# Attention scores of batches 2 to 7 as per-head float32 products on 32x32 array tiles

## The chip, the cores and the metric

The kernel runs on one core of a Trainium2 chip. The metric is device time in microseconds (us) of one execution; lower is better. A core has five engines that work side by side, each on its own in-order list of instructions: PE (TensorE, the matrix engine; PEld is its weight loads), DVE (VectorE), ACT (ScalarE), POOL (GpSimd) and SP (SyncE, which here issues the DMAs). PE multiplies a stationary operand, loaded into a 128x128 array, with a moving operand that streams past it, and writes its sums to PSUM, which has eight banks of 512 float32 words per partition. A smaller product can be placed on part of the array: on a group of rows (the partitions that it reads) and a group of columns (the partitions that it writes).

## The reference

```python
def sm_attn(qq, kk, vv):
    s = scale * np.matmul(qq, kk.transpose(0, 1, 3, 2))
    s = s - np.max(s, axis=-1, keepdims=True)
    a = np.exp(s)
    a = a / (np.sum(a, axis=-1, keepdims=True) + 1e-09)
    return np.matmul(a, vv)
p_packed = sm_attn(p, k, v)              # p: 32 rows per head; q, k, v: 576 rows per head
out = sm_attn(q, p_packed, p_packed)
...
xn = x / rms * rms_g                     # x: 4608 tokens x 512 (8 heads x 64)
y = (silu(xn @ w_gate) * (xn @ w_val)) @ w_out       # 512 -> 1536 -> 512
h = y @ w_in                                         # 512 -> 2048
out = np.maximum(0.01 * h, h) @ w_out2               # 2048 -> 512
```

There are 8 batches and 8 heads of dimension 64. Two products of each head are called scores here: p with k (32 x 576, "s1") and q with the packed result P (576 x 32, "s2").

## The kernel before

Attention is done in 16 units of one batch b and one half u of the heads (four heads). A unit has two parts. `soft1` (s1) loads k and p, turns them on DVE (`keys`, `packs`), makes the scores with PE, then exponents on ACT, and the packed result on PE (`packed`); `packed_turn` turns that for the second part. `soft2` (s2) loads and turns q (`queries`), makes the scores against P and goes on to the attention weights, the squares for the norm and the factors of the first MLP.

The 576 tokens stand as 32 partitions per head and 18 blocks: partition 32h+t holds 18 consecutive tokens of head h. DVE's transpose works on 32x32 blocks in place, so after it partition 32h+d holds dimension d of head h, in two halves j of 32 dimensions. A score contracts over these partitions. Four heads at once on the full array need a block-diagonal stationary operand: `packs` multiplies p by a 0/1 mask on POOL (`pm`) and transposes 128x256; `packed` writes P through a mask to `Pm` and `packed_turn` transposes that to `PT`. The tokens are taken in two chunks c of nine blocks (288 columns), one PSUM bank each, so a score is four float32 matmuls (two chunks by two halves j) of 128x128 by 288 columns (L312 for s1, L470 for s2). A float32 matmul shows in the trace as two records, each with a weight load.

In odd batches the heads of a pair stand swapped: `load_rows` loads them in four DMAs of 32 partitions instead of one. Later steps rely on that order of the output rows.

The first MLP follows in 96 steps of (hidden block, batch of a pair, chunk): g and v (L143, up to six matmuls each per half), then y. These are float32r products in three terms (high and low halves). The attention of later batches is hung into these steps by tables of slot numbers (`ONE`, `TWO`), four slots to a step. Batches 0 and 1 are done ahead of the first step (slots below 0), batches 2 to 7 within the steps. A scheduler then orders each engine's instructions by program order and by its own estimate of when each can start; PSUM tiles of tag "y" (four banks) serve y, the scores, `ta`, `pp` (the packed result) and the `fold` products alike.

`fold` (L888) folds the norm's gain and P into the MLP weights. It already works on small tiles: 64x32, eight at once (four column groups by two row groups), 512 columns, into two banks; `claim` ahead of it writes 16 columns into the first of the two banks (L867), so that the eight start together. `packed` (L367) works on four tiles of 96x32, 64 columns, six products summed on each tile.

The branches for `i >= FAST` and `i >= FASTQ` never run: both are 16 and i ends at 15.

Of the kernel before, what the change touches and what calls it, by code (L numbers as in the profile page):

```python
# [8 lines left out]
F32 = mybir.dt.float32  # L9
# [40 lines left out]
WBUFS = 8  # L50
FAST = 16
FASTQ = 16
OWN = 1
# [15 lines left out]
def pack_attention_moe_kernel(  # L69
# [125 lines left out]
    def load_rows(dst, src, b, u):  # L195
# [5 lines left out]
        return ins  # L201

    raw = {}

    def load_k(b, u):
        t = att.tile([P, NS, 2, T], F32, tag="raw", bufs=raws, name=f"k{b}{u}")
        last = load_rows(t.rearrange("p s j t -> p (s j t)"), kf, b, u)
        tp = att.tile([P, D], F32, tag="praw", bufs=2, name=f"p{b}{u}")
        load_rows(tp, pf, b, u)
        raw["k", b, u] = t  # L210
        raw["p", b, u] = tp
        return last
# [7 lines left out]
    def load_q(b, u):  # L220
        t = att.tile([P, NS, 2, T], F32, tag="raw", bufs=raws, name=f"q{b}{u}")
        load_rows(t.rearrange("p s j t -> p (s j t)"), qf, b, u)
        raw["q", b, u] = t
# [31 lines left out]
    def soft1(i):  # L255
# [4 lines left out]
        def keys():  # L260
            kr = raw.pop(("k", b, u))
            st["kT"] = att.tile([P, NS, 2, T], F32, tag="tr", bufs=2, name="kT" + nm)
            nc.vector.transpose(
                out=st["kT"].rearrange("p s j t -> p (s j t)"),
                in_=kr.rearrange("p s j t -> p (s j t)"),
            )
            if i >= FAST:
                st["kh"] = att.tile([P, NS, 2, T], F32R, tag="raw", bufs=raws, name="kh" + nm)
                st["kl"] = att.tile([P, NS, 2, T], F32R, tag="tr", bufs=2, name="kl" + nm)
                split(st["kT"], st["kh"], st["kl"])  # L270
            if i + 1 < NU:
                last = load_k(*divmod(i + 1, 2))
            if i == 0:
                with tc.issue_after(last.ins):
                    for f_ in weights[HOLD:]:
                        f_()

        def packs():
            pr_ = raw.pop(("p", b, u))
            pm = att.tile([P, 4, D], F32, tag="pm", bufs=1, name="pm" + nm)  # L280
            nc.gpsimd.tensor_tensor(
                out=pm, in0=pr_.unsqueeze(1).to_broadcast([P, 4, D]), in1=mask, op=ALU.mult
            )
            st["pT"] = att.tile([P, 2, 4, NPK], F32, tag="pT", bufs=2, name="pT" + nm)
            nc.vector.transpose(out=st["pT"], in_=pm.rearrange("p h (j d) -> p j h d", j=2))
            if i >= FAST:
                st["ph"] = att.tile([P, 2 * P], F32R, tag="pm", bufs=1, name="ph" + nm)
                st["pl"] = att.tile([P, 2 * P], F32R, tag="pT", bufs=2, name="pl" + nm)
                split(st["pT"].rearrange("p j h k -> p (j h k)"), st["ph"], st["pl"])

        def scores():
            e1 = st["e1"] = att.tile([P, T, NS], F32, tag="e1", bufs=1, name="e1" + nm)
            ev = e1.rearrange("p t (c s) -> p c s t", c=2)
            mx = att.tile([P, 2], F32, tag="mx", bufs=2, name="mx" + nm)
            parts = banks("s1" + nm, b)
            for n, (s1, cs) in enumerate(parts):
                for k_, c in enumerate(cs):
                    if i >= FAST:
                        ss = slice(c * CS, (c + 1) * CS)
                        mm3(  # L300
                            s1[:, k_, :CH],
                            [
                                (
                                    (st["ph"][:, j * P : j * P + P], st["pl"][:, j * P : j * P + P]),
                                    (st["kh"][:, ss, j, :], st["kl"][:, ss, j, :]),
                                )
                                for j in range(2)
                            ],
                        )
                        continue  # L310
                    for j in range(2):
                        nc.tensor.matmul(  # L312
                            s1[:, k_, :CH],
                            lhsT=st["pT"][:, j].rearrange("p h k -> p (h k)"),
                            rhs=st["kT"][:, c * CS : (c + 1) * CS, j, :],
                            start=j == 0,
                            stop=j == 1,
                        )
# [42 lines left out]
        def packed():  # L361
            vr = raw.pop(("v", b, u))
            pp = bank("pp" + nm)
            for j in range(NJ):
# [20 lines left out]

        def packed_turn():
            PT = att.tile([P, 2, 4, NPK], F32, tag="PT", bufs=2, name="PT" + nm)
            Pj = st["Pm"].rearrange("p h (j d) -> p j h d", j=2)
# [5 lines left out]
            raw["P", b, u] = (st["Pm"], PT)  # L394
            if i >= FAST:
                Ph = att.tile([P, 2 * P], F32R, tag="Ph", bufs=2, name="Ph" + nm)
                Pl = att.tile([P, 2 * P], F32R, tag="PT", bufs=2, name="Pl" + nm)
                split(PT.rearrange("p j h k -> p (j h k)"), Ph, Pl)
                raw["P", b, u] = (st["Pm"], (Ph, Pl))

# [19 lines left out]
    def soft2(i):  # L420
# [14 lines left out]
        def queries(cs):  # L435
# [6 lines left out]
            if cs[-1] == 1:  # L442
                raw.pop(("q", b, u))
                if i >= FAST:
                    st["qh"] = att.tile([P, NS, 2, T], F32R, tag="raw", bufs=raws, name="qh" + nm)
                    st["ql"] = att.tile([P, NS, 2, T], F32R, tag="tr", bufs=2, name="ql" + nm)
                    split(qT, st["qh"], st["ql"])
                if i + 1 < NU:
                    load_q(*divmod(i + 1, 2))

        def scores(cs):
            Pm, PT = raw["P", b, u]
            sn = tile_of("sn", "sn", [P, NS, NPK])
            for s2, cs in banks("s2" + nm, b):
                for k_, c in enumerate(cs):
                    if i >= FAST:
                        ss = slice(c * CS, (c + 1) * CS)
                        mm3(
                            s2[:, k_, :CH],
                            [  # L460
                                (
                                    (PT[0][:, j * P : j * P + P], PT[1][:, j * P : j * P + P]),
                                    (st["qh"][:, ss, j, :], st["ql"][:, ss, j, :]),
                                )
                                for j in range(2)
                            ],
                        )
                        continue
                    for j in range(2):
                        nc.tensor.matmul(  # L470
                            s2[:, k_, :CH],
                            lhsT=PT[:, j].rearrange("p h k -> p (h k)"),
                            rhs=st["qT"][:, c * CS : (c + 1) * CS, j, :],
                            start=j == 0,
                            stop=j == 1,
                        )
                nc.vector.transpose(
# [36 lines left out]
        def turn(cs):  # L514
# [4 lines left out]
            )  # L519
            if i >= FASTQ:  # L520
                Pm = raw["P", b, u][0].rearrange("p h d -> p (h d)")
                st["Pm"] = [
                    att.tile([P, 2 * P], F32R, tag="pT", bufs=2, name=f"Pm{x}" + nm) for x in "hl"
                ]
                split(Pm, *st["Pm"])
                st["ATs"] = [
                    att.tile([P, S], F32R, tag="sn", bufs=2, name="ATh" + nm),
                    att.tile([P, S], F32R, tag="sql", bufs=1, name="ATl" + nm),
                ]
                split(AT.rearrange("p s t -> p (s t)"), *st["ATs"])  # L530

        def squares(cs, x):
# [18 lines left out]
            for xp, cs in banks(f"xp{x}" + nm, b):  # L551
                for k_, c in enumerate(cs):
                    if i >= FASTQ:
                        ds, ts = slice(x * P, x * P + P), slice(c * CH, c * CH + CH)
                        ph, pl = st["Pm"]
                        ah, al = st["ATs"]
                        mm3(xp[:, k_, :CH], [((ph[:, ds], pl[:, ds]), (ah[:, ts], al[:, ts]))])
                        continue
                    nc.tensor.matmul(  # L559
# [303 lines left out]
    pw = {}  # L863

    def claim(tiles):
        for t in tiles:
            ins = nc.tensor.matmul(t[:, :16], lhsT=ones, rhs=ones[:, :16], start=True, stop=True)  # L867
        return tc.issue_after(ins.ins) if tiles else nullcontext()

# [604 lines left out]
```

## Time and profile before

| | us |
|---|---|
| median of 3 runs | 1621.32 (1619.37 to 1626.13) |
| profiled execution | 1616.19 |
| its span, first to last instruction | 1614.4 |
| PE busy in the span | 1546.5 (96%) |
| DVE, ACT, POOL busy | 1103.1 (68%), 765.2 (47%), 608.1 (38%) |

The span falls into three stretches: up to 100 us batches 0 and 1 and the loads of the first weights; from 100 to 690 us the first MLP with the attention of batches 2 to 7 hung in; from 690 us the rest of the first MLP and the second one. Busy time counts an engine as long as any instruction of it is open. PE's matmuls overlap, so what a matmul costs the engine is read from the distance between starts and not from its own duration.

### The profile page before, as it was taken

How to read it: one execution, taken by the hardware profiler on the slowest of the kernel's cores; microseconds unless marked ns; L12 is line 12 of the kernel's file. 1: busy time of each engine (PE TensorE's matmuls, PEld its weight loads, DVE VectorE, ACT ScalarE, POOL GpSimd, SP SyncE). 2: the span in 40 equal slices, each digit the busy share in tenths (PEclk: the TensorE clock that was granted, in tenths of full speed). 3: DMA queues.
4: the chain of work that ended last, by engine and by line, in shares of the span. 5: the costliest groups of instructions: out<-in, count | busy, mean ns of one | idle time of the engine just before them, and what ended most of it. 6: DMA issues, size and time to landing. Idle time of an engine off the chain costs nothing.

```text
span 1614.4 us, 28209 instructions
## 1 busy us (share of the span) xinstructions
PE 1546.5 (96%) x10160; PEld 1381.9 (86%) x10160; DVE 1103.1 (68%) x1942; ACT 765.2 (47%) x1390; POOL 608.1 (38%) x427
## 2 busy tenths in 40 slices
PE   6779999999999899999999999999999999999997
PEld 4558889888898788998989888888889998999997
DVE  7887887557766756677777549546854964684485
ACT  3465545464445555446444346346524633553452
POOL 1225343433434534355214562075017306512610
PEclk8899999999999999999999999999999999999999
DMA  8654563465556735559765766787787778778776
GB/s 279 219 180 156 177 202 113 137 221 196 171 184 201 256 120 177 180 189 335 256 240 194 249 203 202 213 282 202 202 270 241 217 225 281 217 216 262 216 216 180
DMA packets 216538, 342.14 MB, mean 212 GB/s; under 512 B 21328, under 2 KB 120656, under 8 KB 216400
## 3 DMA queue, kind: packets, MB, share of 16 engines
q1 hardware_dynamic: 214512, 339.42, 66.9%
q8 instruction: 82, 1.34, 0.3%
q10 hardware_dynamic: 1888, 0.92, 0.3%
q14 instruction: 56, 0.46, 0.1%
HBM read 266.86 MB, written 73.40 MB: 211 GB/s over the span
## 4 chain that ended last, share of the span: by engine, by line
PE 70%; DVE 10%; DMA 10%; ACT 4%; POOL 2%; issue 2%; SPq 1%; ACTq 0%; DVEq 0%; POOLq 0%
PE o L143 22%; PE h L143 20%; PE y L143 12%; PE g L143 5%; PE v L143 5%; DMA sl<-c_dram 1%; PE pwps L888 1%; DMA w<-in_moe_w_out_dram 1%; DVE y_acc L950 1%; PE s L470 1%; PE xp L559 1%; DMA wo<-in_moe_w_out_dram 1%; DMA w<-in_moe_w_val_dram 1%; DMA w<-in_moe_w_in_dram 1%; DMA v<-in_v_dram 1%
## 5 line engine op out<-in xcount | busy, mean ns | idle before, releaser
L143 PE MATMUL o<-gh,pc 128*128 128x448 f32 (+1 forms) x1120 | 323.0, 370 | 0.0
L143 PE MATMUL h<-yh,pc 128*128 128x448 f32 (+1 forms) x1120 | 279.3, 371 | 5.0 <-DMA pc<-s_dram 2.1
L143 PE MATMUL y<-hh,wo 128*128 128x288 f32 x1536 | 274.7, 301 | 7.3 <-ACT y_acc L160 4.2
L143 PEld LDWEIGHTS y<-hh,wo 128*128 128x128 f32 x1536 | 225.5, 189 | 29.5 <-ACT y_acc L160 5.2
L168 POOL TENSOR_TENSOR hl<-sg,hh 128x576 fp32r<-128x576 f32 x96 | 146.6, 1528 | 272.1 <-ACT hh L160 262.6
L143 PEld LDWEIGHTS h<-yh,pc 128*128 128x128 f32 x1120 | 209.6, 188 | 30.4 <-issue 3.2
L143 PEld LDWEIGHTS o<-gh,pc 128*128 128x128 f32 x1120 | 210.2, 188 | 23.0
L160 ACT ACTIVATE gh<-g 128x448 fp32r<-128x448 f32 (+1 forms) x280 | 160.8, 587 | 128.8 <-PE o L143 86.3
L168 DVE TENSOR_TENSOR gl<-g,gh 128x448 fp32r<-128x448 f32 (+1 forms) x280 | 180.3, 662 | 48.3 <-ACT gh L160 44.0
L143 PE MATMUL o<-gl,pc 128*128 128x448 f32 (+1 forms) x560 | 206.4, 370 | 0.0
L1298 POOL TENSOR_TENSOR b6h<-b6h,b5h 128x448 f32<-128x448 f32 (+1 forms) x40 | 59.4, 1485 | 344.0 <-ACT gh L160 289.2
L950 DVE TENSOR_TENSOR y_acc<-y_acc,y 128x288 f32<-128x288 f32 x320 | 139.3, 445 | 62.0 <-PE y L143 61.3
L143 PE MATMUL y<-hl,wo 128*128 128x288 f32 x768 | 164.6, 297 | 1.3 <-POOL hl L168 1.2
L143 PE MATMUL h<-yl,pc 128*128 128x448 f32 (+1 forms) x560 | 162.0, 370 | 0.0
L143 PE MATMUL g<-ath,pw 128*128 128x288 f32 x768 | 154.9, 309 | 5.7 <-ACT pw L160 3.7
L143 PE MATMUL v<-ath,pw 128*128 128x288 f32 x768 | 145.1, 301 | 0.6 <-DVE sg L927 0.5
L143 PEld LDWEIGHTS g<-ath,pw 128*128 128x128 f32 x768 | 116.6, 188 | 28.5 <-issue 10.1
L143 PEld LDWEIGHTS y<-hl,wo 128*128 128x128 f32 x768 | 123.9, 190 | 2.6 <-POOL hl L168 2.6
L1292 POOL TENSOR_TENSOR g<-g,g 128x448 f32<-128x448 f32 (+1 forms) x80 | 116.1, 1451 | 24.9 <-ACT gh L160 13.2
L143 PEld LDWEIGHTS v<-ath,pw 128*128 128x128 f32 x768 | 115.7, 188 | 4.9 <-DVE sg L927 1.5
L143 PEld LDWEIGHTS h<-yl,pc 128*128 128x128 f32 x560 | 105.1, 188 | 11.6
L143 PEld LDWEIGHTS o<-gl,pc 128*128 128x128 f32 x560 | 105.1, 188 | 11.5
(153 smaller groups left out, 2479.1 us busy)
## 6 DMA issues: line engine op xcount, KB each, us to landing
pc<-s_dram SPq DMA_DIRECT2D x320, 256.0 KB, 3.0
pc<-w_dram SPq DMA_DIRECT2D x240, 256.0 KB, 3.0
w<-w_dram SPq DMA_DIRECT2D x72, 256.0 KB, 4.6
wo<-wo_dram SPq DMA_DIRECT2D x36, 512.0 KB, 5.0
w_dram<-w2s SPq DMA_DIRECT2D x32, 512.0 KB, 5.0
s_dram<-ss SPq DMA_DIRECT2D x32, 512.0 KB, 5.8
v<-in_v_dram SPq DMA_DIRECT2D x16, 576.0 KB, 5.3
y_dram<-y_acc SPq DMA_DIRECT2D x32, 288.0 KB, 2.8
```

The source lines that it names most:

```text
L143: mm = nc.tensor.matmul(ps, lhsT=lh if a == "h" else ll, rhs=rh if b == "h" else rl, start=start and i == 0, stop=stop and i == n - 1,)
L160: nc.scalar.activation(out=o, in_=i, func=AF.Copy, scale=scale)
L168: eng.tensor_tensor(out=o, in0=a, in1=hi.bitcast(F32), op=ALU.subtract)
L470: nc.tensor.matmul(s2[:, k_, :CH], lhsT=PT[:, j].rearrange("p h k -> p (h k)"), rhs=st["qT"][:, c * CS : (c + 1) * CS, j, :], start=j == 0 ...
L559: nc.tensor.matmul(xp[:, k_, :CH], lhsT=Pm[:, 2 * x : 2 * x + 2, :].rearrange("p h d -> p (h d)"), rhs=st["AT"][:, c * CS : (c + 1) * CS, ...
L888: return nc.tensor.matmul(ps[32 * h : 32 * h + 32], lhsT=lpw[2 * (n // NFG) + bb][rs, 2 * u + h // 2, c : c + 32], rhs=w[h // 2][rs], star ...
L950: pace[:] = [nc.vector.tensor_tensor(out=ya, in0=ya, in1=pv, op=ALU.add).ins]
L1292: eng.tensor_tensor(out=o, in0=a, in1=b, op=ALU.subtract)
L1298: return eng.tensor_tensor(out=o, in0=a, in1=b, op=ALU.add)
```

## The change

The scores of batches 2 to 7 (b >= HEAD = 2, 12 units, 24 scores) become sixteen float32 products of 32x32 by 288 columns: two halves j, two chunks c, four heads h. Chunk 0 of head h stands on row group h, chunk 1 on row group h^2; both write column group h (h^1 in odd batches), each chunk into its own bank. `claim` goes ahead of them. Since nothing is block-diagonal any more, the mask on POOL goes for p; the DVE transposes work on the bare p and on a scaled copy `Pu` of the packed result, in pieces that move between row groups. `Pm` stays for its other users. k and q are loaded by chunk: chunk 0 in one DMA of 128 partitions, chunk 1 in two DMAs of 64 that swap the row groups; the swap in odd batches is gone from these loads and sits in the output column group. The dead branches are removed (left out below).

```diff
-FAST = 16
-FASTQ = 16
+HEAD = 2
...
+    def rho(c):
+        return 2 * c
+
+    def load_long(t, src, b, u):
+        if b < HEAD:
+            return load_rows(t.rearrange("p s j t -> p (s j t)"), src, b, u)
+        n = CS * D
+        tc_ = t.rearrange("p (c s) j t -> p c (s j t)", c=2)
+        for c in range(2):
+            step = P - 32 * rho(c)
+            for at in range(0, P, step):
+                to, fr = at ^ 32 * rho(c), P * u + at
+                ins = nc.sync.dma_start(
+                    out=tc_[to : to + step, c], in_=src[b, fr : fr + step, c * n : c * n + n]
+                )
+        return ins
...
+    def turned(dst, src, moves):
+        src = src.rearrange("p (j d) -> p j d", j=2)
+        for c, x in enumerate(moves):
+            n = {0: P, 2: 64}.get(x, 32)
+            for at in range(0, P, n):
+                to = at ^ 32 * x
+                nc.vector.transpose(out=dst[to : to + n, c], in_=src[at : at + n])
...
+        todo = [
+            (j, t, k_, c, h)
+            for j in range(2)
+            for t, cs in reversed(out)
+            for k_, c in enumerate(cs)
+            for h in range(4)
+        ]
+
+        def part(j, t, k_, c, h):
+            r, o = 32 * (h ^ rho(c)), 32 * (h ^ b % 2)
+            return nc.tensor.matmul(
+                t[o : o + 32, k_, :CH],
+                lhsT=left[r : r + 32, c, j, :],
+                rhs=right[r : r + 32, c * CS : (c + 1) * CS, j, :],
+                start=j == 0,
+                stop=j == 1,
+            )
+
+        with claim([t[:, 0, :] for t, _ in out[:-1]]):
+            first = part(*todo[0])
+        with tc.issue_after(first.ins):
+            for x in todo[1:]:
+                part(*x)
...
         def packs():
             pr_ = raw.pop(("p", b, u))
+            if b >= HEAD:
+                st["pT"] = att.tile([P, 2, 2, NPK], F32, tag="pT", bufs=2, name="pT" + nm)
+                turned(st["pT"], pr_, [rho(c) for c in range(2)])
+                return
...
         def packed_turn():
+            if b >= HEAD:
+                Pu = att.tile([P, D], F32, tag="Pu", bufs=2, name="Pu" + nm)
+                nc.vector.tensor_scalar(
+                    out=Pu, in0=st["pp"][:, 0, :D], scalar1=st["rin"], scalar2=None, op0=ALU.mult
+                )
+                PT = att.tile([P, 2, 2, NPK], F32, tag="PT", bufs=2, name="PT" + nm)
+                turned(PT, Pu, [b % 2 ^ rho(c) for c in range(2)])
+                raw["P", b, u] = (st["Pm"], PT)
+                return
```

On PE, the s1 score of batch 6 (names: s161_0 and s161_1 are the banks of its chunks, pwps a fold, y the first MLP's output) stands like this before:

```order
L888 MATMUL pwps1300_6068<-w53_5625,lpw4_3391 32x512
L312 MATMUL s161_0_6094<-kT61_6027,pT61_5967 128x288 x2
L312 MATMUL s161_1_6095<-kT61_6027,pT61_5967 128x288 x2
L143 MATMUL y11111_6119<-hh1111_5940,wo22_5230 128x288
L143 MATMUL y11111_6119<-hh1111_5940,wo23_5336 128x288
```

and like this in the changed kernel:

```order
L890 MATMUL pwps1300_6339<-w53_5896,lpw4_3540 32x512
L223 MATMUL s161_0_6365<-ones_97 128x16
L257 MATMUL s161_1_6366<-kT61_6302,pT61_6240 32x288 x4
L257 MATMUL s161_0_6365<-kT61_6302,pT61_6240 32x288 x4
L257 MATMUL s161_1_6366<-kT61_6302,pT61_6240 32x288 x4
L257 MATMUL s161_0_6365<-kT61_6302,pT61_6240 32x288 x4
L142 MATMUL y11111_6403<-hh1111_6215,wo22_5471 128x288
```

Four full-array matmuls became one claim and sixteen tiles in one piece. In 10 of the 24 scores the claim stands right ahead of the tiles as here; in 14 there are 1 to 23 matmuls of the MLP between them. In one score, the s1 of batch 4, nine MLP matmuls stand ahead of the last tile:

```order
L566 MATMUL xp130_1_3132<-AT30_2978,Pm30_2276 128x288
L223 MATMUL s140_0_3142<-ones_97 128x16
L257 MATMUL s140_1_3143<-kT40_3047,pT40_3003 32x288 x4
L257 MATMUL s140_0_3142<-kT40_3047,pT40_3003 32x288 x4
L257 MATMUL s140_1_3143<-kT40_3047,pT40_3003 32x288 x4
L257 MATMUL s140_0_3142<-kT40_3047,pT40_3003 32x288 x3
L142 MATMUL g500_3107<-ath0_546,pw50_2639 128x288
L142 MATMUL g500_3107<-atl0_547,pw50_2639 128x288 x2
L142 MATMUL g500_3107<-ath0_546,pw50_2639 128x288 x4
L142 MATMUL g500_3107<-atl0_547,pw50_2639 128x288 x2
L257 MATMUL s140_0_3142<-kT40_3047,pT40_3003 32x288
```

Here PE leaves the small tiles and comes back to them. On DVE, the turn of the packed result of batch 3 (odd; y_acc adds the MLP's output, cvwo converts weights) now stands as

```order
L419 SCALAR_TENSOR_TENSOR Pm31_2795<-pp31_2770,rin31_2685,swapped_103 128x256
L433 TENSOR_SCALAR Pu31_2854<-pp31_2770,rin31_2685 128x64
L526 TENSOR_SCALAR sm230_2835<-sm230_2835 128x18
L713 SCALAR_TENSOR_TENSOR cvwo10_2800<-wo10_2410,cvwo10_2800 128x512
L952 TENSOR_TENSOR y_acc1_118<-y_acc1_118,y3111_2818 128x288
L232 STREAM_TRANSPOSE PT31_2856<-Pu31_2854 32x64 x2
L527 RECIPROCAL sm230_2835<-sm230_2835 128x18
L232 STREAM_TRANSPOSE PT31_2856<-Pu31_2854 32x64
L952 TENSOR_TENSOR y_acc1_118<-y_acc1_118,y3112_2839 128x288
L232 STREAM_TRANSPOSE PT31_2856<-Pu31_2854 32x64 x5
```

where before two transposes of 128x128 followed `Pm`. `Pu` comes right behind `Pm`, so the bank of `pp` is read twice in a row.

## Rows read from the trace of the kernel before

**Rows 1.** Windows: stretch, length, busy of PE, PEld, DVE, ACT, POOL; clock, DMA share.
```profile
100.00:690.00 590.00, 571.41 (x4714) 512.37 (x4715) 416.98 (x787) 305.49 (x535) 245.45 (x174) 0.99 0.55 178
```

**Rows 2.** Chain of waits, 560 to 600 us: start, us on the chain, what.
```profile
574.02 1.60 PE y L143 x12
...
581.87 1.94 PE s L312 x8
```

**Rows 3.** Groups by line, 100 to 690 us: count, busy us, mean ns, idle before.
```profile
L312 PE MATMUL s<-kT,pT 128*128 128x288 f32 x96 | 26.1, 408 | 1.4 <-DVE pw L168 1.4
L470 PE MATMUL s<-qT,PT 128*128 128x288 f32 x96 | 26.0, 407 | 0.3 <-DVE mx L324 0.3
```

**Rows 4.** Timeline of PE around a fold: start, us, instructions.
```profile
387.59 0.42 PE L143 MATMUL g<-ath,pw 128*128 128x288 f32 x2
387.95 1.09 PE L888 MATMUL pwps<-w,lpw 64*32 64x512 f32 x16
388.96 0.54 PE L143 MATMUL g<-ath,pw 128*128 128x288 f32 x2
389.34 0.43 PE L143 MATMUL g<-atl,pw 128*128 128x288 f32 x2
```

**Rows 5.** Timeline of PE around `packed` and a claim with its fold behind it.
```profile
350.69 0.42 PE L143 MATMUL v<-atl,pw 128*128 128x288 f32 x2
351.04 0.88 PE L367 MATMUL pp<-v,a1T 96*32 96x64 f32 x48
351.85 0.79 PE L143 MATMUL y<-hh,wo 128*128 128x288 f32 x4
352.48 0.42 PE L143 MATMUL y<-hl,wo 128*128 128x288 f32 x2
352.74 0.17 PE L867 MATMUL pwps<-ones 128*128 128x16 f32 x1
352.85 1.09 PE L888 MATMUL pwps<-w,lpw 64*32 64x512 f32 x16
353.87 0.81 PE L143 MATMUL g<-ath,pw 128*128 128x288 f32 x4
354.51 0.43 PE L143 MATMUL g<-atl,pw 128*128 128x288 f32 x2
```

**Rows 6.** Timeline of PE around a claim whose fold comes later.
```profile
364.08 0.69 PE L143 MATMUL v<-ath,pw 128*128 128x288 f32 x4
364.61 0.17 PE L867 MATMUL pwps<-ones 128*128 128x16 f32 x1
364.63 0.52 PE L143 MATMUL v<-atl,pw 128*128 128x288 f32 x2
364.99 0.68 PE L143 MATMUL v<-ath,pw 128*128 128x288 f32 x4
```

**Rows 7.** Groups by line, 100 to 690 us, of the turns around the scores.
```profile
L285 DVE STREAM_TRANSPOSE pT<-pm 128x256 f32<-128x256 f32 x10 | 4.0, 401 | 0.0
L393 DVE STREAM_TRANSPOSE PT<-Pm 128x128 f32<-128x128 f32 x12 | 3.0, 289 | 0.1
L375 DVE SCALAR_TENSOR_TENSOR Pm<-pp,rin,swapped 128x256 f32<-128x256 f32 x6 | 2.9, 480 | 0.9 <-PE pp L367 0.9
L390 DVE STREAM_TRANSPOSE PT<-Pm 128x256 f32<-128x256 f32 x6 | 2.6, 441 | 0.1
L345 DVE TENSOR_SCALAR rin<-sm 128x1 f32<-128x1 f32 x12 | 1.8, 151 | 9.5 <-ACT e L338 9.5
```

**Rows 8.** DMA issues by line: count, KB each, us from issue to landing.
```profile
k<-in_k_dram SPq DMA_DIRECT2D x8, 576.0 KB, 4.2
```

**Rows 9.** Windows around a drop of the granted clock.
```profile
231.00:235.00 4.00, 2.74 (x24) 1.90 (x25) 3.99 (x12) 1.87 (x4) 1.18 (x1) 0.81 0.26 80
235.00:238.00 3.00, 3.00 (x25) 2.95 (x30) 2.14 (x5) 0.68 (x1) 3.00 (x2) 0.68 0.93 274
```

**Rows 10.** Timeline of PE ahead of that drop.
```profile
232.26 1.09 PE L888 MATMUL pwps<-w,lpw 64*32 64x512 f32 x16 [1.71 <-DVE rin L345]
```

More of the change, by code (lines that the diff above doesn't have):

```diff
@@ new lines, in pack_attention_moe_kernel, with claim @@
+    raw = {}
+    def claim(tiles):
+        for t in tiles:
+            ins = nc.tensor.matmul(t[:, :16], lhsT=ones, rhs=ones[:, :16], start=True, stop=True)
+        return tc.issue_after(ins.ins) if tiles else nullcontext()
+    def turned(dst, src, moves):
[5 more added lines that the diff above has]
+                nc.vector.transpose(out=dst[to : to + n, c], in_=src[at : at + n])
@@ new lines, in scores_of @@
+    def scores_of(out, b, left, right):
+        if b < HEAD:
+            for t, cs in out:
+                for k_, c in enumerate(cs):
+                    for j in range(2):
+                        nc.tensor.matmul(
+                            t[:, k_, :CH],
+                            lhsT=left[:, j].rearrange("p h k -> p (h k)"),
+                            rhs=right[:, c * CS : (c + 1) * CS, j, :],
+                            start=j == 0,
[15 more added lines that the diff above has]
+                rhs=right[r : r + 32, c * CS : (c + 1) * CS, j, :],
+                start=j == 0,
+                stop=j == 1,
+            )
[4 more added lines that the diff above has]
+                part(*x)
@@ L205, in load_k @@
     def load_k(b, u):
         t = att.tile([P, NS, 2, T], F32, tag="raw", bufs=raws, name=f"k{b}{u}")
-        last = load_rows(t.rearrange("p s j t -> p (s j t)"), kf, b, u)
+        last = load_long(t, kf, b, u)
         tp = att.tile([P, D], F32, tag="praw", bufs=2, name=f"p{b}{u}")
-        load_rows(tp, pf, b, u)
+        if b < HEAD:
+            load_rows(tp, pf, b, u)
+        else:
+            nc.sync.dma_start(out=tp, in_=pf[b, P * u : P * u + P])
         raw["k", b, u] = t
@@ L295, in scores @@
             parts = banks("s1" + nm, b)
+            scores_of(parts, b, st["pT"], st["kT"])
             for n, (s1, cs) in enumerate(parts):
[L297 to L318, printed above, removed]
                 act_copy(
@@ L362, in packed @@
             vr = raw.pop(("v", b, u))
-            pp = bank("pp" + nm)
+            pp = st["pp"] = bank("pp" + nm)
             for j in range(NJ):
@@ L453, in scores @@
             sn = tile_of("sn", "sn", [P, NS, NPK])
[L454 to L476, printed above, removed]
+            parts = banks("s2" + nm, b)
+            scores_of(parts, b, PT, st["qT"])
+            for s2, cs in parts:
                 nc.vector.transpose(
@@ L863, in pack_attention_moe_kernel @@
     pw = {}
[L865 to L868, printed above, removed]
     def fold(n, u, bbs=(0, 1)):
```

38 lines of the change are left out of this document (3 added, 35 removed).

## The prediction

> **What bounds the kernel now.** I read the windows first, to see which engine fills the stretch in which the changed scores lie. They all lie between 100 and 690 us; there PE is busy for 571.4 of 590 us, at a granted clock of 0.99, while DVE is busy for 417.0, ACT for 305.5 and POOL for 245.5, and the DMA engines for 0.55 of the time [rows 1]. So PE has 18.6 us without work in 590, and work taken off PE should show almost whole in the end time, unless a wait takes its place. Then I read the chain and PE's timeline to learn what a piece of PE work costs as a distance between starts. A float32r matmul of the first MLP, 288 columns, costs 1.60/12 = 0.133 us [rows 2]. The groups by line give the count of what is changed: 96 + 96 records of score matmuls in this stretch, eight to a score, so 24 scores [rows 3].
>
> **PE, the score before.** A score of eight records takes 1.94 us on the chain [rows 2]. That is 0.2425 us for one pass of 288 columns, 0.842 ns a column, and it needs no gap at either end: the MLP's matmuls before and behind it have the same array shape. 24 x 1.94 = 46.6 us.
>
> **PE, the score after.** No 32x32 tile stands in the trace, but `fold` is near: eight 64x32 tiles, two to each column group, two banks, two passes of 512 columns. From the start of the two g matmuls ahead of it to the start of what follows the two g matmuls behind it, 387.59 to 389.34, are 1.75 us [rows 4]; less these four at 0.133 that leaves 1.22 us. If the eight stream together, two passes take 2 x 512 x 0.842 ns = 0.86 us, and 0.36 us are the way into the small tiles and back. One after another they would take 6.9 us, so they do run together. `packed` shows that a longer chain of sums on the same tiles keeps that pace: six products, twelve passes of 64 columns, are 0.65 us by the same rate; 350.69 to 352.48 are 1.79 us less six MLP matmuls (0.80), that is 0.99, again 0.34 for the way in and out [rows 5].
>
> The new score has eight tiles side by side (four heads, two chunks) and four passes behind one another on each (two halves j, two passes each): 4 x 0.2425 = 0.97 us, and 0.36 for the way in and out. To that comes the claim. Where its tiles come later it costs 0.11 us: 364.08 to 364.99 are 0.91 us for six matmuls (0.80) and the claim [rows 6]. Where they follow at once it lies in the way in: from 352.48 to 354.51 are 2.03 us less six matmuls, 1.23 for claim and fold against 1.22 for a fold alone [rows 5]; I take 0.37 for both ends. So a score costs 0.97 + 0.36 + 0.11 = 1.44 us in the 14 cases with matmuls behind the claim and 0.97 + 0.37 = 1.34 in the 10 others. The one score that is torn apart by nine matmuls goes in and out twice, 0.36 more. Sum: 14 x 1.44 + 10 x 1.34 + 0.36 = 33.9 us, and 46.6 - 33.9 = 12.7 us saved. The bounds: with both ends free the saving is 24 x 0.97 = 23.3 us; with tiles that do not overlap it is a loss (rivals).
>
> **DVE.** Each of the 12 units loses a transpose of 128x256 for p and gains three with 64 columns. In even batches the turn of P loses 0.441 us and gains `Pu` and three transposes; in odd ones it loses 2 x 0.289 and gains `Pu` and eight. A transpose of 64 columns does not stand in the trace: 0.289 us at 128 columns and 0.441 at 256 make 1.19 ns a column, so 0.213 at 64; it lies between 0.151 (one column, the smallest DVE instruction here) and 0.289. `Pu` reads PSUM as `Pm` does, which takes 0.480 at 256 columns; between that and 0.151 I set 0.233 [rows 7]. p: 12 x (0.639 - 0.401) = 2.9. Even: 6 x (0.233 + 0.639 - 0.441) = 2.6. Odd: 6 x (0.233 + 1.704 - 0.578) = 8.2. Together 13.6 us more, 7.3 and 21.3 with the two bounds. DVE has 173 us of idle time in the stretch [rows 1], which hides most of this. What is not hidden is a `y_acc` addition or a `pw` split queued behind the eight transposes, for which PE waits. If PE's whole idle time is put down to DVE, 18.6 us for 417.0 of DVE work, 13.6 us bring 0.6; at the other end PE waits for all 13.6. I take 2 us, nearer the first, since PE has four y banks between itself and these additions.
>
> **POOL, ACT, SP.** The mask product leaves POOL, which bounds nothing here; no gain. ACT's copies and DVE's maxima find both chunks ready at about 1.3 us where they had the first at 0.97 and the second at 1.94; no cost, since the second used to come last. The scores need two free y banks at once; the claim waits for the first of them, and that wait is in the 2 us above. Loads: k and q get three DMAs each, instead of one in even and four in odd batches, p one instead of four; SP issues six fewer in all. They are issued about a unit ahead, so 4.2 us of landing [rows 8] are covered; without that cover a late load would cost up to that once per load.
>
> **Sum.** 12.7 - 2 = 10.7 us less, from 1616.2 (the profiled execution's own time) to 1605.5. That execution was 5.1 us below the median; the same difference from the median of 1621.3 gives 1610.6 us. The scheduler puts other instructions into a new order as well. That has no price in the trace; if it moved PE's 18.6 us of idle time by a third either way, 6 us. So 1604 to 1617 for this case.
>
> **Rivals.**
> DVE takes it back. The odd batches' turn puts nine short instructions in DVE's queue, partly among `y_acc` additions. If every added DVE microsecond held up PE, 12.7 - 13.6 makes 1622; with half of them, 1615. For it: DVE is busy for 71% of the stretch, and one wait on `pw` stands right ahead of an s1 score [rows 3]. Against it: 173 us idle. Together with an unlucky order I set 1614 to 1622.
>
> The clock drops (slower). During a score only half of the array's cells work, and 0.36 us go in and out. A drop in the trace follows a wait of PE of 1.71 us [rows 10], and costs 4 x 0.19 + 3 x 0.32 = 1.7 us at the granted clock of 0.81 and 0.68 in those windows [rows 9]. With a drop in every second score, 12 x 1.7 = 20.6, the time is 1631; it decides from seven drops on (10.7/1.7 = 6.3). Against it: folds and `packed` go in and out in the same way, in a stretch at 0.99 [rows 1].
>
> One row group serves one tile at a time (slower). A group of 32 partitions feeds two tiles at once, chunk 0 of one head and chunk 1 of another. If they took turns, a score would take eight passes in a row, 1.94 + 0.36 + 0.11 = 2.41 us, 0.47 more than before, and the time is 1621.3 + 11.3 + 2 = 1635. Against it: in `fold` four tiles of different columns read the same 64 partitions and it still takes 1.22 us [rows 4].
>
> One bank takes one row group at a time (slower). The four tiles of a chunk come from four row groups and write one bank. If these took turns, each bank would see sixteen passes, 3.88 + 0.47 = 4.35 us a score, 24 x 2.41 = 58 us more, 1681. In `fold` each bank is written from two row groups; taking turns it would need 1.72 + 0.36 = 2.08 us, and it needs 1.22 [rows 4]. So two at once are shown, four are not. The Trainium skill states this rule (TensorEngine Tiling (Array Packing), Gotcha 1: PSUM Pressure): different row tiles cannot access the same PSUM bank at the same time. By that rule the time would be the 1681 of this rival; the fold's 1.22 us disagrees with it for tiles of different column groups.
>
> **How the numbers follow.** The runs of before spread by 6.8 us, so a change under 0.5% (8.1 us, 1613.2) is about what can't be told from none. The forecast has 0.66, of which 0.60 lie below 1613.2; DVE or order taking it back 0.24 (0.02 below, 0.20 within, 0.02 above 1629.4); clock 0.04; row group 0.03; bank 0.03, of which 0.08 end slower. So faster 0.62, same 0.28, slower 0.10. The range of 8 in 10 takes in the forecast's own range, the DVE rival up to its end, and part of the way to the bound of free ends (1621.3 - 23.3 = 1598): 1601 to 1622.
>
> **What would show it.** Between PE's start of the first 32x32 tile and the first MLP matmul behind the score there should be about 1.06 us (0.97 and some 0.1 of the way out), with eight tiles started within 0.1 us and the same tiles again every 0.24 us; 2 us or more there would be a rival. DVE's 64-column transposes should take about 0.21 us and DVE's busy time rise by some 14 us. PE's idle time in the stretch should stay near 18.6 us; if it grows by 10, the DVE rival was right. The clock should drop no more than twice in it. The forecast is wrong if the first MLP ends less than 5 us earlier.

## The result and the profile after

The changed kernel takes 1636.35 us (median of 4 runs, 1634.26 to 1637.92), the kernel before 1622.01 beside it (4 runs, 1619.37 to 1626.13). The ratio is 1.0085, 95% interval 1.0061 to 1.011: 13.8 us slower, where 10.7 us faster was forecast. The time lies outside the forecast range. One of the eight runs of a later experiment (e12) took 2864.87 us at a granted clock of 0.858 and is left out of its figures. The profiled execution is one of 1636.23 us, span 1634.5.

The windows of the changed kernel, columns as in [rows 1]:

```profile
100.00:690.00 590.00, 552.75 (x5206) 480.60 (x5205) 420.36 (x848) 302.79 (x533) 235.51 (x162) 0.99 0.54 174
```

PE is busy for 18.7 us less than in [rows 1] and idle for 37.3 us instead of 18.6, at the same clock, and in these 590 us it gets less far. Since a fixed stretch holds different work in the two, I lined both up by the ends of the MLP's Silu: from the 1st to the 73rd, before takes 641.4 us (PE busy 616.9, idle 24.5) and the changed kernel 652.6 (609.4, 43.2). So 7.5 us of busy time went and 18.7 us of waiting came: 11.2 us. Another 4.1 us were lost ahead of the first Silu, where no changed score stands; all the edited kernels below come to it 0.5 to 7.6 us later than the kernel before. The last 4.8 of the 20.1 us between the two spans lie behind the 73rd Silu, 4.5 of them behind the last one, where the two programs do the same work.

Groups by line of the changed kernel, 100 to 690 us, columns as in [rows 3]; the first two answer to [rows 3], the third is the claims, the last three answer to [rows 7]:

```profile
L257 PE MATMUL s<-kT,pT 32*32 32x288 f32 x384 | 15.1, 407 | 1.1 <-DVE y_acc L952 0.6 <-ACT sq L573 0.3
L257 PE MATMUL s<-qT,PT 32*32 32x288 f32 x352 | 13.2, 407 | 1.5 <-DVE y_acc L952 0.9 <-DVE pw L167 0.3 <-ACT y_acc L159 0.3
L223 PE MATMUL s<-ones 128*128 128x16 f32 x23 | 4.7, 205 | 0.8 <-DVE mx L368 0.6 <-DVE y_acc L952 0.2
L232 DVE STREAM_TRANSPOSE PT<-Pu 32x64 f32<-32x64 f32 (+2 forms) x66 | 15.7, 237 | 1.1
L232 DVE STREAM_TRANSPOSE pT<-p 64x64 f32<-64x64 f32 (+1 forms) x30 | 6.8, 227 | 0.3
L433 DVE TENSOR_SCALAR Pu<-pp,rin 128x64 f32<-128x64 f32 x12 | 3.3, 275 | 0.0
```

The scores themselves wait for little (1.1 and 1.5 us). What waits is the MLP. PE's waits between 95 and 740 us, by what waits and for whom (us in total, times, longest); before:

```profile
PE y L143 <- DVE pw L168: 2.0, 3, 1.0
PE g L143 <- ACT sg L1238: 1.1, 2, 0.9
PE y L143 <- DVE mx L324: 0.3, 1, 0.3
```

and changed:

```profile
PE y L142 <- DVE pw L167: 13.6, 13, 2.6
PE g L142 <- ACT sg L1240: 5.2, 5, 1.7
PE y L142 <- DVE mx L368: 1.8, 2, 1.0
```

A `y` product needs one of the four y banks, and `pw` is the fold's split, which frees a bank. This one wait grew by 11.6 us, the largest part of the 18.7. One place shows how such a wait comes about. Timeline of PE before:

```profile
323.35 0.69 PE L143 MATMUL v<-ath,pw 128*128 128x288 f32 x4
323.88 2.10 PE L312 MATMUL s<-kT,pT 128*128 128x288 f32 x8
325.60 0.65 PE L143 MATMUL g<-atl,pw 128*128 128x288 f32 x2
326.09 0.69 PE L143 MATMUL g<-ath,pw 128*128 128x288 f32 x4
326.61 0.43 PE L143 MATMUL g<-atl,pw 128*128 128x288 f32 x2
326.88 0.42 PE L143 MATMUL v<-atl,pw 128*128 128x288 f32 x2
327.14 0.69 PE L143 MATMUL v<-ath,pw 128*128 128x288 f32 x4
327.66 0.29 PE L143 MATMUL v<-atl,pw 128*128 128x288 f32 x1
328.98 0.53 PE L143 MATMUL y<-hh,wo 128*128 128x288 f32 x2 [1.02 <-DVE pw L168]
```

and the `pw` split of DVE that it waits for:

```profile
328.25 0.68 DVE L168 TENSOR_TENSOR pw<-pwps,pw 128x512 fp32r<-128x512 f32 x1
```

The same place in the changed kernel, PE:

```profile
333.00 0.28 PE L223 MATMUL s<-ones 128*128 128x16 f32 x1
333.13 0.78 PE L142 MATMUL g<-ath,pw 128*128 128x288 f32 x4
333.75 0.69 PE L142 MATMUL v<-ath,pw 128*128 128x288 f32 x4
334.36 1.20 PE L257 MATMUL s<-kT,pT 32*32 32x288 f32 x32
335.49 0.53 PE L142 MATMUL g<-atl,pw 128*128 128x288 f32 x2
335.86 0.69 PE L142 MATMUL g<-ath,pw 128*128 128x288 f32 x4
336.39 0.42 PE L142 MATMUL g<-atl,pw 128*128 128x288 f32 x2
336.65 0.29 PE L142 MATMUL v<-atl,pw 128*128 128x288 f32 x1
339.59 0.66 PE L142 MATMUL y<-hh,wo 128*128 128x288 f32 x3 [2.65 <-DVE pw L167]
```

and DVE and ACT beside it:

```profile
332.63 0.75 DVE L696 TENSOR_SCALAR cvw<-cvw 128x512 f32<-128x512 f32 x2
333.29 3.22 DVE L702 TENSOR_SCALAR cvw<-cvw 128x512 uint32<-128x512 uint32 x2
336.44 2.49 DVE L713 SCALAR_TENSOR_TENSOR cvw<-w,cvw 128x512 uint32<-128x512 uint32 x2
338.86 0.68 DVE L167 TENSOR_TENSOR pw<-pwps,pw 128x512 fp32r<-128x512 f32 x1
...
341.25 0.44 DVE L368 TENSOR_REDUCE mx<-s 128x1 f32<-128x288 f32 x1
```

```profile
334.11 1.07 ACT L159 ACTIVATE pw<-pwps 128x512 fp32r<-128x512 f32 x2
335.60 0.71 ACT L159 ACTIVATE e<-s 128x288 f32<-128x288 f32 x1 [0.42 <-PE s L257]
340.16 0.63 ACT L159 ACTIVATE w2s<-cvw 128x512 fp32r<-128x512 f32 x1 [3.85 <-DVE cvw L719]
340.70 0.69 ACT L159 ACTIVATE e<-s 128x288 f32<-128x288 f32 x1
```

From the start of the score to the `pw` split's end are 5.05 us before (323.88 to 328.93) and 5.18 after (334.36 to 339.54): DVE keeps its pace. PE does its score in 1.13 us there instead of 1.72, has nine MLP matmuls to do behind it where there were fifteen, and then stands for 2.65 us instead of 1.02. Two of the four y banks hold the fold, whose `pw` splits stand behind four conversions in DVE's queue. The other two hold the score: the first from the claim at 333.00 to the end of the maximum at 341.69, the second until after that, since ACT's second copy stands behind a `w2s` copy that waits for DVE. I added up this time, first product into a bank to the end of its last reader, over the 12 first and the 12 second scores of batches 2 to 7. Before, a pair of scores holds its banks for 13.8 us (8.33 + 5.51, both banks added), changed for 18.8 (10.96 + 7.80). Of the 4.9 us that came, 2.2 lie between the claim and the first tile (1.03 and 1.21 us a score, in the first bank), 2.1 between the end of the filling and the end of the last reader, and 0.6 in the filling, since both banks are now filled at once.

### The profile page after: what moved, and what is told of

The parts are those of the page before. It is cut to its first block, busy times and chain, and to the rows that moved or that the text cites. A ratio compares the mean times of both kernels' runs of the same rounds, so it can differ in the third digit from the quotient of the medians.

```text
span 1634.5 us, 29463 instructions
## 1 busy us (share of the span) xinstructions
PE 1547.3 (95%) x10760; PEld 1363.4 (83%) x10760; DVE 1117.9 (68%) x2026; ACT 764.7 (47%) x1390; POOL 598.5 (37%) x415
## 4 chain that ended last, share of the span: by engine, by line
PE 66%; DVE 14%; DMA 9%; ACT 4%; issue 3%; POOL 2%; SPq 1%; ACTq 0%; DVEq 0%; POOLq 0%
PE o L142 22%; PE h L142 20%; PE y L142 11%; PE g L142 5%; PE v L142 4%; DMA sl<-c_dram 2%; DVE y_acc L952 2%; DMA wo<-in_moe_w_out_dram 2%; DMA w<-in_moe_w_in_dram 1%; PE pwps L890 1%; DMA w<-in_moe_w_out_dram 1%; PE xp L566 1%; DMA pc<-s_dram 1%; DVE pw L167 1%; DVE cvw L713 1%
## 5 line engine op out<-in xcount | busy, mean ns | idle before, releaser
L142 PE MATMUL y<-hh,wo 128*128 128x288 f32 x1536 | 274.0, 301 | 20.4 <-DVE pw L167 13.6
L142 PEld LDWEIGHTS h<-yl,pc 128*128 128x128 f32 x560 | 105.1, 188 | 12.3
L142 PEld LDWEIGHTS o<-gl,pc 128*128 128x128 f32 x560 | 105.1, 188 | 12.3
```

The lines of the kernel that those rows point to most:

```text
L142: mm = nc.tensor.matmul(ps, lhsT=lh if a == "h" else ll, rhs=rh if b == "h" else rl, start=start and i == 0, stop=stop and i == n - 1,)
```

## The experiments

Costs are against the kernel before, from the ratio of runs on the same chip, with the 95% interval. "Idle" is PE's idle time in the window from 100 to 690 us, 18.6 before and 37.3 in the changed kernel; it is one execution each.

**Added work of DVE, and loads.** Changed kernel, one transpose for each turn:

```diff
-        for c, x in enumerate(moves):
+        for c, x in enumerate([0]):
...
-                lhsT=left[r : r + 32, c, j, :],
+                lhsT=left[r : r + 32, 0, j, :],
```

> The changed kernel with the DVE turns cut down: one transpose of 64 columns for p and one for the packed result in each unit of batches 2 to 7, instead of three and three or eight; chunk 1 takes the stationary operand of chunk 0 (so the scores of chunk 1 are not the reference's). PE's, SP's and POOL's work is that of the changed kernel; DVE's falls by about 16 us. Theory DVE (the added short transposes sit in DVE's queue ahead of pw splits and y additions for which PE waits): the 12.7 us saved on PE appear, 1609 to 1616 us. Theory loads (the split k and q loads delay the weights behind them in SP's queue): 1632 to 1637, as the changed kernel. Theory order (the slot tables fit the old kernel, any new order of the engines' queues costs PE waits): 1625 to 1637.

Measured: 1634.67 us, ratio 1.0102 (1.0063 to 1.014), 16.6 us slower than before; DVE's busy time fell from 420.4 to 409.2 us in the window, idle 32.7. Taking the added transposes out brings nothing that shows; an order drawn anew (below) could hide some us of it. The counterpart, the kernel before with dummy turns:

```diff
+            if b >= 2:
+                dm = att.tile([P, 2, 2, NPK], F32, tag="dm", bufs=2, name="dp" + nm)
+                nc.vector.transpose(out=dm[:, 0], in_=pr_.rearrange("p (j d) -> p j d", j=2))
...
+                Pu = att.tile([P, D], F32, tag="Pu", bufs=2, name="Pu" + nm)
```

> The kernel before plus DVE work of about the size that the change adds, as dummies that nothing reads: one 64-column transpose behind the turn of p, and behind that of the packed result the scaled copy and one transpose (even batches) or five (odd ones), some 13 us in all. PE, POOL and SP do the work of before. Theory DVE: 1632 to 1638. Theory loads: 1621 to 1625. Theory order: 1624 to 1634, since the scheduler reorders here too.

Measured: 1629.41 us, ratio 1.005 (1.0025 to 1.0076), 8.1 us slower. Added to the kernel before this work costs something; taken out of the changed one it brings nothing. Then the loads: the changed kernel with one transfer each for k and q (a line put into `load_long`), and the kernel before with transfers of the changed kernel's sizes, not swapped, for k and q and one for p:

```diff
+        return nc.sync.dma_start(out=t.rearrange("p s j t -> p (s j t)"), in_=src[b, P * u : P * u + P])
```

> The changed kernel with each k and q load of batches 2 to 7 as one DMA of 128 partitions; chunk 1's rows are then not swapped, so its scores are not the reference's. All else as changed. Theory loads: the 4 us before the first MLP step and part of the rest come back, 1624 to 1631. Theory DVE: 1633 to 1637. Theory order: 1628 to 1640.

```diff
-        last = load_rows(t.rearrange("p s j t -> p (s j t)"), kf, b, u)
+        last = load_long(t, kf, b, u)
...
```

> The kernel before with the changed kernel's loads: k and q of batches 2 to 7 in three DMAs, p in one; the head swap of odd batches is left out of the loads, so odd batches are not the reference's. Theory loads: 4 us late at the first MLP step and 1627 to 1634 in the end. Theory DVE: 1620 to 1624. Theory order: 1622 to 1632.

Measured: 1634.37 us, ratio 1.0076 (1.0052 to 1.0101), and 1622.13 us, 0.9993 (0.9972 to 1.0014). The loads cost nothing that can be told.

**Is PE the bound, and what do the banks and the order cost?** The kernel before with half of each score; with both banks claimed; the changed kernel with half of each score; the kernel before with its scores one slot later:

```diff
-                    for j in range(2):
+                    for j in range(1 if b >= 2 else 2):
...
```

> The kernel before, but each score of batches 2 to 7 leaves out its second half (j = 1): four records of 0.2425 us instead of eight, 24 x 0.97 = 23.3 us less PE work between 100 and 690 us, on the full array, with no claim, no added turn and no other loads. Three theories. BANKS (the changed score takes two of the four y banks at once and keeps them longer, and y products wait for a bank): here each bank is kept for less time, so the saved PE time shows, about 1600 us. ORDER (any change of PE time makes the scheduler lay the queues out anew, and the table of slots fits only the old order, 8 to 13 us): 1608 to 1613. PACE (at the folds PE waits for DVE anyway, and PE time taken off becomes waits): 1618 to 1625, and the idle time of PE between 100 and 690 rises by some 20 us.

```diff
+        todo = [(j, t, c) for j in range(2) for t, cs in reversed(out) for c in cs]
...
+        with claim([t[:, 0, :] for t, _ in out[:-1]]):
+            first = part(*todo[0])
```

> The kernel before with full-array scores, but in batches 2 to 7 the score claims both y banks at its start, as the changed kernel does (a 16-column product into the first bank, then for each half j first chunk 1 and then chunk 0), so that both banks come free only behind the whole score. PE work grows only by the claims, 24 x 0.11 = 2.6 us. BANKS: the loss of the changed kernel without its gain, 1633 to 1640, and y products wait for pw more often than the 3 times and 2.0 us of before. ORDER: the order shifts by the claims alone, somewhere from 1626 to 1636. PACE: 1623 + 2.6 or less, 1622 to 1627.

```diff
-            for j in range(2)
+            for j in range(1)
...
```

> The changed kernel, but each score of batches 2 to 7 leaves out its second half (j = 1): two passes on each tile instead of four, 24 x 0.485 = 11.6 us less PE work, and both banks are free 0.49 us earlier. BANKS: the PE time comes off and the waits for banks shrink with it, 1620 to 1625. ORDER: 1635 less 11.6 with an order drawn anew, 1620 to 1632. PACE: PE time taken off becomes waits, 1632 to 1637.

```diff
+        if b >= 2:
+            at[2] += 1
...
+            when[1] += 1
```

> The kernel before with nothing added or left out: the scores of batches 2 to 7 (both kinds) stand one slot later in the table that places them among the MLP's matmuls. BANKS and PACE: no change that can be told, 1619 to 1627. ORDER: the table is fitted so closely that one slot costs 5 to 13 us, 1628 to 1636.

Measured: e6 1608.58 us, 0.9902 (0.9873 to 0.9931), 15.9 us faster. e7 1633.02 us, 1.0059 (1.0037 to 1.0082). e8 1630.68 us, 1.0035 (1.0016 to 1.0053), 8.1 us less than the changed kernel's 13.8. e9 1635.13 us, 1.0067 (1.0045 to 1.0089), 10.9 us slower with the same instructions. Windows of e6 and e9:

```profile
100.00:690.00 590.00, 566.51 (x4747) 508.72 (x4732) 428.81 (x806) 313.66 (x546) 253.06 (x179) 0.99 0.55 181
```

```profile
100.00:690.00 590.00, 562.41 (x4657) 501.58 (x4650) 411.64 (x772) 311.78 (x538) 243.85 (x172) 1.00 0.54 174
```

PACE falls as the whole cause: 23.3 us of PE work taken off bring 15.9, and 11.6 off the changed kernel bring 8.1, some 70% each time by the medians. A part of what is saved does turn into waiting with no bank claimed: PE idles for 23.5 us in e6. ORDER is seen: one slot makes PE's idle time 27.6 us with not one instruction more. e7 speaks against held banks as a cause by themselves. From start to start its scores and claims take 46.4 us where the scores took 41.2, so 5.2 of its 9.6 us are PE time (2.8 of them the claims). Its banks, counted as above from the claim on, are held for 18.3 us a pair, nearly as long as in the changed kernel. Yet PE idles for only 20.8 us in the window, and `y` waits for `pw` no longer than before:

```profile
PE y L143 <- DVE pw L168: 2.1, 4, 0.9
```

**Neighbouring places in the table.** Scores of batches 2 to 7 one slot earlier or later (`at[2] -= 1` or `+= 1`, and the second score alike): the changed kernel earlier, later, the kernel before earlier, and the first experiment's kernel later.

> The changed kernel, with the scores of batches 2 to 7 one slot earlier in the table. ORDER (the table of slots is fitted to the kernel before, so any other order costs it some 10 us; the changed kernel already pays that): the shift is only another unfitted order, so the time moves by no more than 5 us either way, 1630 to 1641, and may as well fall as rise. BANKS (both y banks taken at once): no change that can be told, 1633 to 1638.

> The changed kernel, with the scores of batches 2 to 7 one slot later in the table. ORDER: as for one slot earlier, 1630 to 1641, either way; since it is the edit that cost the kernel before 11 us, another rise by 11 us, to 1646, would say that the place one slot later is bad in itself and not that the old order was fitted. BANKS: 1633 to 1638.

> The kernel before, with the scores of batches 2 to 7 one slot earlier. ORDER: the old place is a fitted one, so the other neighbour costs as well, 1628 to 1637. If instead only later is bad (the softmax behind the score then comes too late), earlier costs nothing: 1618 to 1626.

> The changed kernel with one 64-column transpose for each turn in place of three to eight (chunk 1 then multiplies chunk 0's stationary operand, so it leaves the rearranged copy out), and the scores of batches 2 to 7 one slot later. ORDER alone: 1630 to 1641 like the shift without this edit. If DVE's 15 us of added work cost something that an unlucky order hid in the earlier run of this edit (1634.7), this one comes out 4 to 8 us below the shift without it.

Measured: 1654.19 us, 1.0185 (1.0154 to 1.0215); 1655.55, 1.0192 (1.016 to 1.0223); 1636.30, 1.0076 (1.0048 to 1.0103); 1644.85, 1.0122 (1.0081 to 1.0163). I was wrong that the changed kernel already pays for an unfitted place: both its neighbours cost it another 16 to 17 us. The present slot is the best of three for both kernels, and the changed kernel is the slower one at each: by 13.8, 17.7 and 20.3 us. So the loss is not one badly placed slot; a table drawn anew for the changed kernel was not tried. In the last run the added turns do cost 11 us, at a slot where everything is late.

**Both costs together, and the banks relieved.** The kernel before with both banks claimed and the dummy turns (the edits of e7 and e2); then, in the changed kernel and in the kernel before, the maximum of the first score taken from ACT's copy:

```diff
-                nc.vector.reduce_max(mx[:, n : n + 1], s1[:, :, :CH], axis=AX.XY, negate=True)
+                if b < 2:
+                    nc.vector.reduce_max(mx[:, n : n + 1], s1[:, :, :CH], axis=AX.XY, negate=True)
...
+            if b >= 2:
+                nc.vector.reduce_max(st["nb"], e1, axis=AX.XY, negate=True)
+                return
```

> The kernel before, full-array scores, with two of the changed kernel's side effects and without its tiles: both y banks claimed at the start of a score (10 us by itself) and some 13 us of added VectorE work (8 us by itself). QUEUE (VectorE and the held banks are the cost, and add up): 1623 + 10 + 8, 1636 to 1648; the changed kernel is that less the part of its 12 us that shows. ORDER (each edit pays once for leaving the fitted order, whatever it is): no more than the dearer of the two, 1630 to 1637.

> The changed kernel, but in batches 2 to 7 the maximum of the first score is taken by one VectorE instruction from ScalarE's copy in SBUF, not by two from the y banks, so a bank is free when ScalarE has copied it; VectorE also loses some 4 us of work. QUEUE: each of the 12 first scores gives its banks back about 0.5 to 1 us earlier, and fewer y products wait: 1635 less 4 to 10, 1625 to 1631. ORDER: an order drawn anew, 1630 to 1645, and the same edit costs the kernel before as well.

> The kernel before with the same edit (maximum of the first score from ScalarE's copy, batches 2 to 7). QUEUE: the kernel before waits little for banks, so 0 to 4 us less, 1617 to 1624. ORDER: leaving the fitted order costs 5 to 13 us, 1628 to 1636.

The last one joins this edit with those of e1 and e3:

> The changed kernel with both relieved: the maximum from ScalarE's copy, and one 64-column transpose for each turn (chunk 1 multiplies chunk 0's stationary operand, so the rearranged copy is left out), and k and q loaded by one transfer each (so chunk 1 reads keys and queries of another head). VectorE then has about 3 us less work than in the kernel before. QUEUE: only the claim of both banks is left of the cost, so most of the saved TensorE time shows, 1612 to 1622. ORDER: 1628 to 1640.

Measured: e14 1633.77 us, 1.0078 (1.0053 to 1.0103); e15 1626.67, 1.0028 (1.0009 to 1.0047); e16 1628.96, 1.0037 (1.0009 to 1.0066); e17 1627.57, 1.0034 (1.0011 to 1.0057). The two costs do not add up: 12.7 us where 8.1 and 9.6 make 17.7. The one edit brings the changed kernel 9.3 us (13.8 to 4.5; the intervals lie apart) and costs the kernel before 6.0, though there too it shortens DVE's work and the holding of banks (10.8 us a pair). In e16 `y` waits longer for `pw` than in the kernel before, so this wait does not follow the holding alone:

```profile
PE y L143 <- DVE pw L168: 6.4, 5, 2.5
```

In e15 a pair holds its banks for 14.5 us instead of 18.8. The windows of e15 and its wait for `pw`:

```profile
100.00:690.00 590.00, 558.90 (x5279) 485.90 (x5280) 429.12 (x839) 309.19 (x541) 239.74 (x165) 1.00 0.55 178
```

```profile
PE y L142 <- DVE pw L167: 6.7, 6, 2.6
```

Half of that wait is gone, and PE idles for 31.1 us instead of 37.3. e17 takes DVE's added work out as well and gains no more, as e1 did.

**Two tries to go further**, on the kernel of e15: the second score copied out of its banks by ACT too, and the claim left out.

```diff
+                for s2, cs in parts:
+                    act_copy(sc[:, cs[0] : cs[0] + 1], s2[:, :, :CH])
```

> The changed kernel with the maximum taken from ScalarE's copy (1626.7), and in batches 2 to 7 the second score too is copied out of its banks by ScalarE and turned by VectorE from SBUF, one transpose of 576 columns instead of two of 288 from the y banks. QUEUE: what keeps the banks is VectorE's queue; the second score's banks, held 7.6 us a score in sum, come free when ScalarE has copied them, some 2 us earlier in sum, so 3 to 6 us less, 1620 to 1624. If ScalarE's 24 added copies hold up its own work (Silu, pw), it is no faster: 1626 to 1634. ORDER: 1622 to 1634.

```diff
-        with claim([t[:, 0, :] for t, _ in out[:-1]]):
-            first = part(*todo[0])
+        first = part(*todo[0])
```

> The changed kernel with the maximum taken from ScalarE's copy (1626.7), without the claim: a score no longer takes its first bank with a small product of its own ahead, so 24 x 0.11 = 2.6 us less TensorE work, and the first bank is held some 0.7 us less in the scores with MLP products behind the claim. QUEUE: 3 to 6 us less, 1620 to 1624. If TensorE now stands inside the score until the second bank is free, what the claim filled with MLP products becomes idle time: 1627 to 1633.

Measured: 1630.79 us, 1.0045 (1.0028 to 1.0062), and 1634.66 us, 1.0078 (1.0052 to 1.0105). The copies free nothing (7.71 us a second score, 7.58 without them): the banks now wait for ACT, as a new row of e18's waits shows.

```profile
PE y L142 <- DVE pw L167: 5.9, 5, 2.6
PE y L142 <- ACT sc L159: 4.8, 3, 3.1
```

Without the claim the time rises by some 8 us, but not by waiting: from the 1st to the 73rd Silu PE is idle for 29.5 us in e19 against 37.3 in e15, and busy for 617.0 against 604.1. In 11 of the 24 scores the two chunks now run apart, and such a half takes 1.10 us to the next product, about what the whole score takes (1.13). PE in e19:

```profile
113.04 1.17 PE L257 MATMUL s<-kT,pT 32*32 32x288 f32 x16
114.14 0.40 PE L142 MATMUL g<-ath,pw 128*128 128x288 f32 x1
```

So the claim is what keeps the eight tiles together, and e19 does not tell what the claim costs in held banks. No version of the changed kernel beats the kernel before.

## Why the prediction was wrong

**PE's score: right.** The first tile starts 1.13 us ahead of the next product in 20 of the 24 scores (334.36 to 335.49 above; 1.06 forecast), the four passes some 0.24 us apart; in three others PE waits behind the tiles, and one is the torn score. To that come 0.09 us on the way in and 0.10 on the way out, where the second MLP matmul starts 0.24 us after the first and not 0.13 (the 1.94 of before holds 0.22 of this kind). With 0.12 for the claim a score costs 1.44 us, as forecast, and 1.33 where the claim stands right ahead and nothing waits; the second piece of the torn score costs 0.80 more. 14 x 1.44 + 10 x 1.33 + 0.80 = 34.3 us against 33.9 forecast and 46.6 before: 12.3 us saved, 12.7 forecast. By the rule that I cited from the Trainium skill (TensorEngine Tiling (Array Packing), Gotcha 1: PSUM Pressure) a score would have taken 4.35 us; the trace disagrees, for four tiles on four row groups write one bank at once.

**DVE's work: right in size.** Transposes of 64 columns take 0.23 us and `Pu` 0.275, where 0.213 and 0.233 were set. From the first Silu to the 73rd DVE is busy for 13.1 us more (457.9 to 471.0), 13.6 forecast. Its effect is less clear: nothing in e1 and e17, 11 us one slot later.

**The clock: right to leave out.** The mean is 0.99 in both, with two drops between 100 and 690 us in each.

**The step that failed** is the term of 2 us for all waits. It took in the need for "two free y banks at once", and beside it stands the sentence that ACT's copies and DVE's maxima find both chunks ready at about 1.3 us: "no cost, since the second used to come last". I asked when the data is ready and not when the bank is free. In place of the 2 us PE's idle time grew by 18.7 us where it was to stay near 18.6, and 11.6 of them are `y` products that wait for `pw`. That PE comes to its next `y` sooner and then stands until a bank is free is shown. Why so many banks are taken is shown in part only. For the score's own two banks speaks e15: they are let go 4.3 us a pair sooner, the wait is halved, and 9.3 us come back. But e7 holds its banks as long with full-array scores and waits 2.1 us, and e16 holds them for less than the kernel before and waits 6.4. So a long hold alone does not make the wait, and how much of it is the new order of the queues stays open.

**The second error** is the price of the order, 6 us either way. Beyond what it adds or takes on PE, each edit of the kernel before that moved work on PE or DVE cost something: 8.1 (e2), 7.4 (e6: 23.3 less 15.9), 4.4 (e7), 10.9 (e9), 12.3 (e12), 7.5 (e14), 6.0 us (e16). That is 4 to 12 us by the medians, each give or take some 4, and never a gain, also where the edit takes work away. The edit that moved only loads (e4) cost none. The 18.6 us of idle time belong to the order that this kernel has, and a price "a third either way" should have been one-sided.

**The account.** 12.3 us were saved on PE and 13.8 lost in the end, so 26 us were given back. Some 8 of them (4 to 12) are what any edit paid, and 9 are what e15 gets back by freeing the first score's banks, though an order drawn anew may be part of those 9, and DVE's 4 us less work too. The other 9 us are open: relieving DVE (e17) and copying the second score out of its banks (e18) did not find them, and e19 could not test the claim. The criterion that I had named, idle time growing by 10 for the rival "DVE takes it back", was met, and would have misled: PE does wait for DVE, but taking the added work out did not end the wait (`y` for `pw` 10.5 us in e1).

## What to carry to other kernels

When an engine that fills 97% of a stretch gets a faster step, ask for each buffer behind the step when its readers let it go: a shorter fill does not shorten the hold. If four buffers feed the engine and two jobs may hold two each, saved time can turn into waiting. And where the work is placed by a table, move one entry of the old kernel by one slot first: that price (here 11 to 12 us) is what a new version must beat before its gain can show.

## What the runs showed of the hardware

Some of DVE's conversions take up to four times their usual time beside a POOL instruction: 4 of the 25 of one line take 1.25 to 1.66 us, the others 0.38 to 0.43. That line and shape in the changed kernel, 100 to 690 us, with ns as min/median/max:

```profile
L702 DVE TENSOR_SCALAR cvw<-cvw x25: 378/426/1662, 333.3 to 679.8; 128x512 uint32<-128x512 uint32 x25
```

The two at 333.29 took 3.22 us, and POOL's subtractions lie right over them:

```profile
333.14 3.09 POOL L167 TENSOR_TENSOR atl<-atf,ath 128x576 fp32r<-128x576 f32 x2 [3.12 <-ACT ath L159]
```

The Trainium skill (SBUF — State Buffer, section "SBUF: two separate sides") says that VectorE and GpSimd share a pair of ports which one instruction holds to its end; the trace agrees, each of the two ending 0.29 us after a POOL instruction that ran beside it (3.22 us for the two, 3.09 for POOL's two). In this place it makes the `pw` split behind them late, and in the kernel before likewise (two conversions at 322.09 take 3.14 us).

The two readers of a score's bank do not overlap: DVE's maximum waits for ACT's copy of the same bank, for 14.5 us in the window, as the idle time in its row says, so a bank is held for the sum of both.

```profile
L368 DVE TENSOR_REDUCE mx<-s 128x1 f32<-128x288 f32 x24 | 10.4, 433 | 14.5 <-ACT e L159 14.5
```

Eight tiles of 32x32, two on each of four row groups and four in each bank, keep the pace of a full-array pass, 0.24 us for 288 columns.
